# A folding row moved from step 3 to step 4 in an attention and mixture-of-experts kernel, and three smaller edits

## The chip, the cores and the metric

The kernel runs on one core of a Trainium2 chip. The metric is the device time of one execution in microseconds. The engines are TensorE (PE, with its weight loads as PEld), VectorE (DVE), ScalarE (ACT), GpSimd (POOL) and SyncE (SP), which issues most DMAs. Each engine works through its own instructions in order; semaphores hold an instruction until what it needs is there.

## What is computed

Two softmax attentions in a row, through 32 packed rows for each head, and behind them a mixture of four experts:

```python
# q, k, v: (8, 8, 576, 64), p: (8, 8, 32, 64)
p_packed = sm_attn(p, k, v)             # softmax(p k^T / 8) v
attn = sm_attn(q, p_packed, p_packed)   # softmax(q p_packed^T / 8) p_packed
x = attn.transpose(0, 2, 1, 3).reshape(8 * 576, 512)
dp = domain_probs / (domain_probs.sum(-1, keepdims=True) + 1e-09)
out = 0
for e in range(4):                      # w1: (4, 512, 1024), w2: (4, 1024, 512)
    out += dp[:, e:e + 1] * (np.maximum(x @ w1[e], 0.0) @ w2[e])
```

## The kernel before

**Numbers in two parts.** The matmuls run on fp32 values split in a high part (a cast on ACT, L105) and a low part (value minus high part, L109, on DVE or POOL). A product of two such values is three matmuls: high by high and the two mixed ones.

**Folding.** The second attention's output is a softmax matrix times the 32 packed values of each head, and the next step multiplies it by `w1`. The kernel multiplies the packed values by `w1` first. `g_form` (L294) does that for one chunk of 512 hidden columns and for two batches: per pair of heads (g = 0, 1) one matmul group L76 (`wraw` holds `w1`, `ppbd` the packed values) into one PSUM buffer that holds both batches, then, for each batch, the high part on ACT and the low part on DVE, into an SBUF tile `ghl`. Such a step is called a folding row or a fold; a *joined* fold does g = 0 and g = 1 in one stretch of PE and takes two PSUM buffers, otherwise there are two rows with one buffer each.

**Units.** The work behind it is 64 units u: four sweeps (`sb`) of two batches each, eight chunks (`ch`) in a sweep, the two batches in turn. So sweeps begin at u = 0, 16, 32 and 48. A unit runs seven steps i = 0 to 6 (L657 to L692). Each step has a product: 12 matmuls of the unit's second matrix multiplication in a Strassen form with seven products (`product`, L459), added into `acc` i on DVE (L477). With it comes an operand for a product two steps later (`s_operand`, L365): an add on DVE for some (`sblk`, L375), a high part on ACT, a low part on POOL (`st`). At i = 1, 3, 4 and 6 a *group* of 12 matmuls of the next unit's first matrix multiplication follows (`mm1_groups`, L357, operands `xh`, `xl`, `ghl`), read out by DVE (L350, rectified and weighted, into `ablk`). Behind it, at some steps, a fold is done.

**What sets the order.** PE's order is written out by the code. All of `dbl`, the products, the groups, the folds, and attention's scores and transposes, take turns in one pool of four PSUM buffers (L54), so the fifth taker waits until the first buffer has been read out. The order of the other engines between fixed points is found by a scheduler from the program's dependencies, when the kernel is built; `after` (L59) pins one instruction behind another on an engine. At run time each engine keeps to that order.

**Attention for the next sweep** (scores L76 with `kt`, `pt`; transposes L71; softmax on DVE and ACT; `back`, L680) is spread over the units of the present sweep, at even steps, behind the fold of the same step. At the end of a sweep the seven accumulators are combined (L508, on DVE and POOL) and stored, spread over the next unit's steps (`sums`, L683).

**The folds' places now** (L633 to L637 and L669): from u = 4 on, in every even unit. In the first sweep there are two rows, behind the groups of steps 3 and 6, except u = 14, which prepares the second sweep and is joined, behind step 6. From u = 16 to u = 58 all are joined, behind the group of step 3. u = 60 is joined, behind step 0. The tiles `ghl` come from five buffers, every sixth from a sixth one (`ghl6`, L288).

**The end.** The last unit forms its result by quarters (`quadrant`, L438). The last quarter, (1, 1), is stored in two halves j = 0 and 1 (L451, L452), both out of one PSUM tile.

Of the kernel before, what the change touches and what calls it, by code (L numbers as in the profile page):

```python
# [9 lines left out]
F32R = mybir.dt.float32r  # L10
# [6 lines left out]
P = 128  # L17
# [4 lines left out]
NG = NPAIR // 2  # L22
SB = B // 2
HS = S // 2
FC = 512
NCH = E * F // FC
# [14 lines left out]
def attention_moe(ctx: ExitStack, tc: tile.TileContext, q, k, v, p, dp, w1, w2, out):  # L41
    nc = tc.nc

    def pool(name, bufs=1, **kw):
        return ctx.enter_context(tc.tile_pool(name=name, bufs=bufs, **kw))
# [4 lines left out]
    gpool = pool("gpool")  # L50
# [8 lines left out]
    def after(ins, prev):  # L59
        tc.add_manual_dep(ins, prev.name, nosync, reason="order on an engine")  # L60
# [6 lines left out]
    def mm(**kw):  # L67
        on_pe(nc.tensor.matmul(**kw))  # L68
# [15 lines left out]
    def dbl():  # L84
        return ps_dbl.tile([P, 2, 512], F32, name="dbl")
# [12 lines left out]
    def cols(b, hh):  # L98

        i = (hh + b) % 2  # L100
        return slice(i * NPK, (i + 1) * NPK)

    def hi_of(dst, src, eng):
        if eng is nc.scalar:
            return nc.scalar.copy(out=dst, in_=src)  # L105
        return eng.tensor_copy(out=dst, in_=src)
# [116 lines left out]
    marks = {}  # L223
# [59 lines left out]

    gs = {}

    ring = {"n": 0}

    def ghl_tile():  # L288
        n, ring["n"] = ring["n"], ring["n"] + 1
        if n % 6 == 0:  # L290
            return glast.tile([P, 2, FC], F32R, name="ghl6")
        return gpool.tile([P, 2, FC], F32R, name="ghl", bufs=5)

    def g_form(bs, ch, raws, rows=None, tile=lambda: gpool.tile([P, 2, FC], F32R, name="ghl", bufs=5)):  # L294

        for gr in rows or [[g] for g in range(NG)]:
            pss, calls = {}, []
            for g in gr:
                ps = dbl()
                pss.update({(b, g): ps[:, b % 2] for b in bs})  # L300
                for hs in range(4):
                    pr, hh = 2 * g + hs // 2, hs % 2
                    part = slice(hh * D, (hh + 1) * D)
                    for b in bs:
                        c0 = (hs // 2) * 2 * NPK + cols(b, hh).start
                        calls.append(dict(
                            out=pss[b, g][c0:c0 + NPK, :], lhsT=ppbd[b % 4][part, pr, cols(b, hh)],
                            rhs=raws[pr][part, :], start=True, stop=True,
                        ))
            together(calls)  # L310
            for b in bs:
                for g in gr:
                    ghl = tile()
                    hi_of(ghl[:, 0, :], pss[b, g], nc.scalar)
                    marks[b, ch, g, "low"] = lo_of(ghl[:, 1, :], pss[b, g], ghl[:, 0, :], nc.vector).ins
                    gs.setdefault((b, ch), []).append(ghl)
            yield
# [5 lines left out]
    AHEAD = LAST - 3  # L323
# [114 lines left out]
    def quadrant(r, n):  # L438
        sb, ch, b = units[LAST]
        right = ((0, "b12"), (6, 5))  # L440
        ps = dbl()
        t = accs[b, ORDER.index({(0, 0): "a12", (0, 1): "s4", (1, 0): "a22", (1, 1): "s1"}[r, n])]
        for j in range(2):
            terms = [(k, fi, tl, sl) for k in range(2) for fi in range(2) for tl, sl in ((0, 0), (1, 0), (0, 1))]
            for m, (k, fi, tl, sl) in enumerate(terms):
                mm(
                    out=ps[:, j, 0:HS], lhsT=tt[ch, right[k][n]][:, tl, fi, j * P:(j + 1) * P],
                    rhs=blocks[LAST, "op", 2 * r + k][:, sl, fi, :], start=m == 0, stop=m == len(terms) - 1,
                )
            if (r, n) == (1, 1):  # L450
                nc.vector.tensor_tensor(out=t[:, j], in0=ps[:, j, 0:HS], in1=t[:, j], op=ALU.add)  # L451
                (nc.sync, nc.scalar)[j].dma_start(  # L452
                    out=out[n * DH + j * P:n * DH + (j + 1) * P, b * S + r * HS:b * S + (r + 1) * HS], in_=t[:, j],
                )
        if (r, n) != (1, 1):
            nc.vector.tensor_tensor(out=t, in0=ps[:, :, 0:HS], in1=t, op=ALU.add)
            store(b, t, r, n)
# [72 lines left out]
    def drain(gen):  # L530
        for _ in gen:
            pass
# [5 lines left out]
    with ExitStack() as first:  # L538
# [20 lines left out]
        raws = w1_load(0)  # L559
# [18 lines left out]
        raws = w1_load(1)  # L578
# [34 lines left out]
    for u, (sb, ch, b) in enumerate(units):  # L613
        odd = b % 2 == 1
        nxt = units[u + 1] if u + 1 < len(units) else None

        step = 2 * ch + b % 2
        if sb + 1 < SB:
            pair = [2 * sb + 2, 2 * sb + 3]
            for at_step, make, g in AT_FIRST if sb == 0 else AT_LATER:  # L620
                if at_step == step:
                    drain(back)
                    back = make(pair, g, att_tile, relief=sb == 0)

        gsteps = nothing
        nsb, nch = (sb, ch + 1) if ch + 1 < NCH else (sb + 1, 0)
        if u == 0:
            gsteps = g_form([0], 1, raws)
        elif u == 2 or u == 3:
            gsteps = g_form([1] if u == 2 else [0, 1], u - 1, raws)  # L630
            drain(gsteps)
            raws = w1_load(u)
        elif 3 < u <= AHEAD and not odd and nsb < SB:  # L633
            whole = dict(rows=[range(NG)]) if nsb > 0 else {}
            if sb > 0:
                whole["tile"] = ghl_tile
            gsteps = g_form([2 * nsb, 2 * nsb + 1], nch, raws, **whole)  # L637
        if u == 2 * NCH - 1:
            later.close()
            glast = later.enter_context(tc.tile_pool(name="glast", bufs=1, reuse_waits="tile"))  # L640
        elif u == LAST - 1:
            extra = plain_operand(NCH - 1)
            next(extra)
        elif u == LAST:
            for _ in combine(b, SUMS_LAST):
                pass
            for r in range(2):
                for n in range(2):
                    quadrant(r, n)
                    if r == 0:  # L650
                        s_operand(u, LA + n)
            break
        forming = u == 0 or u > 2 and odd and sb == 0 and ch + 1 < NCH
        if forming:
            tsteps = t_form(ch + 1, raw_tile, {"t1": nc.gpsimd, "t2": nc.vector, "t3": nc.vector, "t4": nc.gpsimd})
            next(tsteps)
        for i in range(NPROD):  # L657
            product(u, i)
            n = i + LA
            if n < NPROD:  # L660
                s_operand(u, n)
            elif nxt:
                s_operand(u + 1, n - NPROD)
            if nxt:
                for grp in (GROUPS_LATE if u in (1, AHEAD) else GROUPS_LAST if u == LAST - 1 else GROUPS).get(i, ()):
                    mm1_groups(u + 1, [grp])
            if u == 0:
                drain(gsteps)
            elif i in ((0,) if u == AHEAD else (6,) if u == 2 * NCH - 2 else (3, 6)):  # L669
                next(gsteps, None)  # L670
            if u == 1 and i == 3:
                drain(second)
                drain(g_form([1], 0, raws))
                raws = w1_load(1)
            for _ in range(SECOND[u][i] if u in SECOND and i < len(SECOND[u]) else 0):
                next(second, None)
            if i == 4 and u > 1 and u + 2 < len(units) and units[u + 2][1] % 2 == 0:
                load_probs(units[u + 2][2], units[u + 2][1] // 2)
            if i % 2 == 0 or sb == 0 and step >= AT_FIRST[2][0]:
                next(back, None)  # L680
            if sb == 0 and i in (FORM_ODD if odd or u == 0 else FORM_EVEN):
                next(tsteps, None)
            next(sums, None)  # L683
            if sb == 0 and not odd:
                t_store(ch, i)
            if u == LAST - 1:
                if i == 1:
                    next(extra)
                elif i in (0, 5, 6):
                    t_load(nxt[1], i)  # L690
            elif nxt and not forming and nxt[1] != ch:
                t_load(nxt[1], i)  # L692
        drain(gsteps)
        drain(sums)
        if ch == NCH - 1:
            sums = combine(b, SUMS)
        if u == 0:
            raws = w1_load(0)
            load_probs(1, 0)
        elif not odd and u > 2:  # L700
            nsb, nch = (sb, ch + 2) if ch + 2 < NCH else (sb + 1, ch + 2 - NCH)
            if nsb < SB:
                raws = w1_load(nch)
# [34 lines left out]
```

## Time and profile before

| | |
|---|---|
| median of three runs | 1296.7 us (1296.26 to 1297.26) |
| profiled execution | 1296.23 us |
| its span, first to last instruction | 1294.4 us |
| DVE busy | 954.9 us (74%) |
| POOL busy | 859.3 us (66%) |
| ACT busy | 493.3 us (38%) |
| PE line of the products, L68 dbl<-st,tt | 5388 matmuls, 772.2 us busy |
| PE line of the folds, L76 dbl<-wraw,ppbd | 1024 matmuls, 69.6 us busy |
| chain that ended last | PE 82%, POOL 7%, DVE 6%, DMA 3%, issue 2%, ACT 1% |

The busy time of an engine says only how much work it has. What a change can win or lose is read from where PE waits, and from what ends that wait. In a timeline row stand the start in us, the duration, the engine, the line, the operation, the written and the read tile with their shapes, how many instructions are drawn together, and in brackets how long the engine was idle before and what ended that idle time.

### The profile page before, as it was taken

To read this page: it belongs to the slowest core of one execution; us is meant where nothing else is said; L and a number is where in the kernel's file an instruction comes from. 1 tells how busy PE (TensorE), PEld (TensorE's weight loads), DVE (VectorE), ACT (ScalarE), POOL (GpSimd) and SP (SyncE) were. 2 spreads that over 40 slices of the span, in tenths; PEclk is the share of its full clock that TensorE was granted. 3 is DMA by queue.
4 is the path that set the end of the run, shared out by engine and by line. 5 is a ranking of instruction groups with operands and counts; after the bars stand their busy time and mean duration, and the time that the engine had idled before them with its cause. 6 is when DMAs were issued, how large, how long until landed. Compare 5 with 4: busy or idle time off the path is not lost.

```text
span 1294.4 us, 26901 instructions
## 1 busy us (share of the span) xinstructions
PE 1265.8 (98%) x10776; PEld 1179.6 (91%) x10776; DVE 954.9 (74%) x1304; ACT 493.3 (38%) x884; POOL 859.3 (66%) x570
## 2 busy tenths in 40 slices
PE   7899999999999999999999999999999999999998
PEld 4689999998889999999999999999999999999998
DVE  6786677899975666897686666799669566766776
ACT  3445545646344333333324423333323533332321
POOL 4778888798985444666578454466567755555565
PEclk9999999999999999999999999999999999999999
DMA  9885656544365544544345546434436443443562
GB/s 351 308 294 195 219 169 228 181 148 167 141 234 198 157 157 129 191 161 156 126 138 187 179 142 201 139 130 124 156 124 202 155 135 115 128 153 130 169 210 97
DMA packets 91707, 223.93 MB, mean 173 GB/s; under 512 B 9280, under 2 KB 32192, under 8 KB 91584
## 3 DMA queue, kind: packets, MB, share of 16 engines
q1 hardware_dynamic: 90768, 221.92, 51.4%
q8 instruction: 86, 1.41, 0.5%
q10 hardware_dynamic: 816, 0.30, 0.1%
q14 instruction: 37, 0.30, 0.1%
HBM read 183.31 MB, written 38.87 MB: 172 GB/s over the span
## 4 chain that ended last, share of the span: by engine, by line
PE 82%; POOL 7%; DVE 6%; DMA 3%; issue 2%; ACT 1%; SPq 0%; DVEq 0%; POOLq 0%; ACTq 0%
PE dbl L68 76%; PE dbl L76 5%; POOL st L109 3%; POOL tt L109 2%; DVE sblk L375 2%; DVE ablk L350 1%; DVE ghl L109 1%; DMA xl<-in_q 1%; POOL b L412 1%; POOL acc L508 1%; DVE a L264 1%; PE dbl L71 1%; DMA vt<-in_v 1%; DMA kt<-in_q 0%; DVE acc L477 0%
## 5 line engine op out<-in xcount | busy, mean ns | idle before, releaser
L68 PE MATMUL dbl<-st,tt 128*128 128x288 f32 x5388 | 772.2, 297 | 7.1 <-POOL st L109 2.1
L68 PEld LDWEIGHTS dbl<-st,tt 128*128 128x128 f32 x5388 | 730.1, 188 | 48.2 <-issue 27.4
L109 POOL TENSOR_TENSOR st<-sblk,st 128x576 fp32r<-128x576 f32 x252 | 393.6, 1569 | 234.4 <-ACT st L105 192.4
L68 PE MATMUL dbl<-xh,ghl 128*128 128x288 f32 x2048 | 415.8, 295 | 5.8 <-DVE ghl L109 3.5
L109 POOL TENSOR_TENSOR st<-ablk,st 128x576 fp32r<-128x576 f32 x193 | 291.0, 1511 | 152.5 <-ACT st L105 151.1
L477 DVE TENSOR_TENSOR acc<-dbl,acc 128x576 f32<-128x576 f32 x385 | 288.3, 752 | 113.7 <-PE dbl L68 113.2
L68 PEld LDWEIGHTS dbl<-xh,ghl 128*128 128x128 f32 x2048 | 328.3, 188 | 7.6 <-DVE ghl L109 4.4
L350 DVE SCALAR_TENSOR_TENSOR ablk<-dbl,pbt 128x576 f32<-128x576 f32 x256 | 192.4, 753 | 156.0 <-PE dbl L68 151.6
L68 PE MATMUL dbl<-xl,ghl 128*128 128x288 f32 x1024 | 300.9, 294 | 1.0 <-DVE xl L109 1.0
L105 ACT CAST st<-sblk 128x576 fp32r<-128x576 f32 x252 | 170.3, 676 | 298.4 <-DVE sblk L375 205.7
L105 ACT CAST st<-ablk 128x576 fp32r<-128x576 f32 x193 | 130.3, 675 | 264.4 <-PE dbl L68 242.2
L68 PEld LDWEIGHTS dbl<-xl,ghl 128*128 128x128 f32 x1024 | 192.1, 188 | 1.4 <-DVE xl L109 1.4
L375 DVE TENSOR_TENSOR sblk<-ablk 128x576 f32<-128x576 f32 x126 | 126.1, 1001 | 9.2
L105 ACT CAST ghl<-dbl 128x512 fp32r<-128x512 f32 x128 | 72.7, 586 | 84.6 <-PE dbl L76 51.9
L109 DVE TENSOR_TENSOR ghl<-dbl,ghl 128x512 fp32r<-128x512 f32 x128 | 85.1, 684 | 11.0 <-ACT ghl L105 8.5
L375 DVE TENSOR_TENSOR sblk<-ablk,sblk 128x576 f32<-128x576 f32 x63 | 69.8, 1107 | 5.7
L76 PE MATMUL dbl<-wraw,ppbd 64*32 64x512 f32 x1024 | 69.6, 596 | 0.4 <-DMA wraw<-in_w 0.3
L109 POOL TENSOR_TENSOR tt<-b,tt 128x512 fp32r<-128x512 f32 x42 | 62.2, 1489 | 2.1 <-ACT tt L105 2.0
L375 DVE TENSOR_TENSOR sblk<-sblk,ablk 128x576 f32<-128x576 f32 x63 | 57.7, 915 | 1.7
L508 POOL TENSOR_TENSOR acc<-acc,acc 128x576 f32<-128x576 f32 x28 | 47.0, 1686 | 11.4 <-DVE acc L477 11.4
L475 ACT COPY acc<-dbl 128x576 f32<-128x576 f32 x56 | 35.9, 640 | 46.4 <-PE dbl L68 46.3
L508 DVE TENSOR_TENSOR acc<-acc,acc 128x576 f32<-128x576 f32 x28 | 39.1, 1400 | 4.9 <-POOL acc L508 4.6
(91 smaller groups left out, 432.9 us busy)
## 6 DMA issues: line engine op xcount, KB each, us to landing
tt<-td SPq DMA_DIRECT2D x192, 512.0 KB, 4.2
wraw<-in_w SPq DMA_DIRECT2D x136, 256.0 KB, 3.8
td<-tt SPq DMA_DIRECT2D x56, 512.0 KB, 3.5
pbt<-pnd SPq DMA_DIRECT2D x32, 288.0 KB, 4.1
out<-acc SPq DMA_DIRECT2D x31, 288.0 KB, 2.3
kt<-in_k SPq DMA_DIRECT2D x14, 576.0 KB, 5.3
kt<-in_q SPq DMA_DIRECT2D x14, 576.0 KB, 5.4
vt<-in_v SPq DMA_DIRECT2D x15, 512.0 KB, 5.3
```

The lines of the kernel that those rows point to most:

```text
L68: on_pe(nc.tensor.matmul(**kw))
L71: on_pe(nc.tensor.transpose(**kw))
L76: ins = nc.tensor.matmul(**kw).ins
L105: return nc.scalar.copy(out=dst, in_=src)
L109: return eng.tensor_tensor(out=dst, in0=src, in1=hi.bitcast(F32), op=ALU.subtract)
L264: marks[b, g, "mul"] = eng.tensor_tensor(out=a2, in0=a2, in1=s2.broadcast_to([P, S // 32, NPK]), op=ALU.mult).ins
L350: nc.vector.scalar_tensor_tensor(out=a, in0=ps[:, :, 0:HS], scalar=0.0, in1=pbt[b][:, c * HS:(c + 1) * HS].rearrange("p (o t) -> p o t", o ...
L375: nc.vector.tensor_tensor(out=t, in0=blk(x), in1=blk(y), op=op)
L412: eng[m].tensor_tensor(out=blk[place], in0=blk[x], in1=blk[y], op=ALU.subtract)
L475: nc.scalar.copy(out=accs[b, i], in_=psv)
L477: nc.vector.tensor_tensor(out=accs[b, i], in0=psv, in1=accs[b, i], op=ALU.add)
L508: eng.tensor_tensor(out=m[dst], in0=m[x], in1=m[y], op=op)
```

## The change

From u = 18 to u = 58 the joined fold is done behind the group of step 4 instead of step 3. In u = 14 and u = 16 it is no longer joined: two rows, behind the groups of steps 3 and 6. Within a fold the high and low parts are now issued with g outside and the batch inside, and the tile that goes to `ghl6` is given by the fold's turn instead of a counter. In u = 12, one multiplication of attention's softmax is pinned behind the low part of a fold. In the last quarter, the second half gets a PSUM tile of its own.

```diff
-    def ghl_tile():
-        n, ring["n"] = ring["n"], ring["n"] + 1
-        if n % 6 == 0:
+    def g_tile(kept=False):
+        if kept:
             return glast.tile([P, 2, FC], F32R, name="ghl6")
         return gpool.tile([P, 2, FC], F32R, name="ghl", bufs=5)
...
-            for b in bs:
-                for g in gr:
-                    ghl = tile()
+            tiles = {(b, g): g_tile((b - bs[0], g) == kept) for b in bs for g in gr}
+            for g in gr:
+                for b in bs:
+                    ghl = tiles[b, g]
                     hi_of(ghl[:, 0, :], pss[b, g], nc.scalar)
...
         for j in range(2):
+            if (r, n, j) == (1, 1, 1):
+                ps = dbl()
...
-            whole = dict(rows=[range(NG)]) if nsb > 0 else {}
+            how = {}
             if sb > 0:
-                whole["tile"] = ghl_tile
-            gsteps = g_form([2 * nsb, 2 * nsb + 1], nch, raws, **whole)
+                turn = (u - 2 * NCH) // 2
+                how["kept"] = (1, 0) if turn == 0 else (None, (0, 1), (1, 1))[(turn - 1) % 3]
+                if turn > 0:
+                    how["rows"] = [range(NG)]
+            gsteps = g_form([2 * nsb, 2 * nsb + 1], nch, raws, **how)
...
-            elif i in ((0,) if u == AHEAD else (6,) if u == 2 * NCH - 2 else (3, 6)):
+            elif i in ((0,) if u == AHEAD else (4,) if u > 2 * NCH else (3, 6)):
                 next(gsteps, None)
...
         drain(gsteps)
+        if u == 12:
+            after(marks[2, 1, "mul"], marks[0, 7, 0, "low"])
```

How that moves instructions is shown at u = 36, in the third sweep. Two lines taken out ahead of these places make line 375 into 373 and line 350 into 348 in the changed kernel. First DVE. Before, from the eviction of the group of step 3 (L350) on: one add, the four low parts with accumulation 4 among them, the eviction of the group of step 4, two adds, then the maxima of attention's scores (L172).

```order
L350 SCALAR_TENSOR_TENSOR ablk<-dbl,pbt 128x576
L375 TENSOR_TENSOR sblk<-ablk 128x576
L109 TENSOR_TENSOR ghl<-dbl,ghl 128x512
L109 TENSOR_TENSOR ghl_9764<-dbl,ghl_9764 128x512
L109 TENSOR_TENSOR ghl<-dbl,ghl 128x512
L477 TENSOR_TENSOR acc_8779<-dbl,acc_8779 128x576
L109 TENSOR_TENSOR ghl<-dbl,ghl 128x512
L350 SCALAR_TENSOR_TENSOR ablk<-dbl,pbt 128x576
L375 TENSOR_TENSOR sblk<-ablk 128x576
L375 TENSOR_TENSOR sblk<-sblk,ablk 128x576
L172 TENSOR_REDUCE nb<-dbl 128x1 x2
L176 TENSOR_SCALAR nb<-nb 128x1
```

Now, from the same eviction on:

```order
L348 SCALAR_TENSOR_TENSOR ablk<-dbl,pbt 128x576
L373 TENSOR_TENSOR sblk<-ablk 128x576
L477 TENSOR_TENSOR acc_8749<-dbl,acc_8749 128x576
L348 SCALAR_TENSOR_TENSOR ablk<-dbl,pbt 128x576
L373 TENSOR_TENSOR sblk<-ablk 128x576
L373 TENSOR_TENSOR sblk<-sblk,ablk 128x576
L109 TENSOR_TENSOR ghl<-dbl,ghl 128x512 x4
L172 TENSOR_REDUCE nb<-dbl 128x1 x2
L176 TENSOR_SCALAR nb<-nb 128x1
L477 TENSOR_TENSOR acc_8814<-dbl,acc_8814 128x576
```

The four low parts have moved behind the eviction of the group of step 4 and behind two adds instead of one, in front of L172. The `acc` rows count from accumulation 4 (8779 before, 8749 now) to accumulation 5 (8814).

On PE at the same fold, from its last two matmuls on (`ppbd_83` and `ppbd_84` are the packed values of the two batches, `xh_6608` and `xl_6609` the high and low part of a group's operand, `kt,pt` attention's scores). Before, product 4 and its group follow:

```order
L76 MATMUL dbl<-wraw,ppbd_83 32x512
L76 MATMUL dbl<-wraw,ppbd_84 32x512
L68 MATMUL dbl<-st,tt 128x288 x12
L68 MATMUL dbl<-xh_6608,ghl 128x288 x2
L68 MATMUL dbl<-xl_6609,ghl 128x288
```

Now the scores follow, then products 5 and 6, then the group of step 6:

```order
L76 MATMUL dbl<-wraw,ppbd_83 32x512
L76 MATMUL dbl<-wraw,ppbd_84 32x512
L76 MATMUL dbl<-kt,pt 32x288 x16
L68 MATMUL dbl<-st,tt 128x288 x24
L68 MATMUL dbl<-xh_6608,ghl 128x288 x2
```

What attention puts at step 4 of a unit, scores here and transposes in others, used to stand one product and one group behind the fold and now stands straight behind it.

More of the change, by code (lines that the diff above doesn't have):

```diff
@@ L284, in attention_moe, with g_form @@
     gs = {}
-    ring = {"n": 0}
-    def ghl_tile():
-        n, ring["n"] = ring["n"], ring["n"] + 1
-        if n % 6 == 0:
+    def g_tile(kept=False):
+        if kept:
             return glast.tile([P, 2, FC], F32R, name="ghl6")
         return gpool.tile([P, 2, FC], F32R, name="ghl", bufs=5)
-    def g_form(bs, ch, raws, rows=None, tile=lambda: gpool.tile([P, 2, FC], F32R, name="ghl", bufs=5)):
+    def g_form(bs, ch, raws, rows=None, kept=None):
         for gr in rows or [[g] for g in range(NG)]:
```

## The prediction

> **What bounds the kernel now.** I read the page first, then what TensorE waited for, then the order of events around single folds, because the change moves folds.
>
> ```profile
> span 1294.4 us, 26901 instructions
> PE 1265.8 (98%) x10776; PEld 1179.6 (91%) x10776; DVE 954.9 (74%) x1304; ACT 493.3 (38%) x884; POOL 859.3 (66%) x570
> PEclk9999999999999999999999999999999999999999
> ```
>
> PE is busy for 98% of the span and its clock is full in every slice. PE is the path: 28.6 us (1294.4 - 1265.8) are all that moving work could give, and any new wait of PE is paid in full. The change adds or drops no instruction of PE's arithmetic, so the forecast is a sum of waits. From 300 us on, where the change acts, PE waited for:
>
> ```profile
> PE dbl L68 <- DVE ghl L109: 2.9, 2, 1.7
> PE dbl L68 <- issue: 1.7, 2, 1.1
> PE dbl L68 <- DVE ablk L350: 1.5, 1, 1.5
> PE dbl L68 <- DVE nb L176: 0.9, 1, 0.9
> ```
>
> (total, times, longest, in us). These are few. Below I price a wait by the start-to-start time of PE's groups against an undisturbed one, which is slightly more than the idle time that a row shows.
>
> **A fold now and later, at a plain place.** This is the fold of u=50, at step 3, with no attention work near it:
>
> ```profile
> 1045.68 1.95 PE L76 MATMUL dbl<-wraw,ppbd 64*32 64x512 f32 x32
> 1045.79 0.76 DVE L350 SCALAR_TENSOR_TENSOR ablk<-dbl,pbt 128x576 f32<-128x576 f32 x1 [0.84 <-PE dbl L68]
> 1046.65 0.76 DVE L375 TENSOR_TENSOR sblk<-ablk 128x576 f32<-128x576 f32 x1
> 1047.56 1.87 PE L68 MATMUL dbl<-st,tt 128*128 128x288 f32 x12
> 1049.27 0.43 PE L68 MATMUL dbl<-xh,ghl 128*128 128x288 f32 x2
> 1050.87 2.29 PE L68 MATMUL dbl<-st,tt 128*128 128x288 f32 x16
> ```
>
> Call the fold's start F. The fold takes 1.88 us (1047.56 - 1045.68), the product behind it 1.71, the group 1.60. A fold fills two of the four PSUM buffers, so the third 12-matmul piece behind it takes the fold's first buffer again and must wait until both low parts in it are made. Now that is product 5, at F+5.19. On DVE, eviction L350 runs at F+0.11, one add L375 from F+0.97 to F+1.73, then the lows. How they follow one another in the g-first order, which the change writes down, is seen at u=36, together with what comes behind:
>
> ```profile
> 776.37 0.69 DVE L109 TENSOR_TENSOR ghl<-dbl,ghl 128x512 fp32r<-128x512 f32 x1
> 777.10 1.08 ACT L105 CAST ghl<-dbl 128x512 fp32r<-128x512 f32 x2 [0.76 <-DVE ghl L109]
> 777.72 1.29 DVE L109 TENSOR_TENSOR ghl<-dbl,ghl 128x512 fp32r<-128x512 f32 x2 [0.65 <-ACT ghl L105]
> 779.80 1.20 PE L76 MATMUL dbl<-kt,pt 64*32 64x288 f32 x32
> 780.93 3.47 PE L68 MATMUL dbl<-st,tt 128*128 128x288 f32 x24
> 781.12 1.19 DVE L375 TENSOR_TENSOR sblk<-ablk 128x576 f32<-128x576 f32 x1
> 783.09 1.42 DVE L172 TENSOR_REDUCE nb<-dbl 128x1 f32<-128x576 f32 x2
> 785.28 0.53 PE L68 MATMUL dbl<-xh,ghl 128*128 128x288 f32 x2 [0.88 <-DVE nb L176]
> ```
>
> The second cast waits for the first low (777.10 behind 776.37 + 0.69), the second low starts 1.35 us behind the first, the third 0.65 later. At step 4 the new DVE order has group 4's eviction and then **two** adds ahead of the lows. Two such adds of one step, undisturbed, stand at u=20:
>
> ```profile
> 469.33 0.76 DVE L375 TENSOR_TENSOR sblk<-ablk 128x576 f32<-128x576 f32 x1
> 469.49 3.47 PE L68 MATMUL dbl<-st,tt 128*128 128x288 f32 x24
> 470.19 0.76 DVE L375 TENSOR_TENSOR sblk<-sblk,ablk 128x576 f32<-128x576 f32 x1
> 473.06 0.54 PE L68 MATMUL dbl<-xh,ghl 128*128 128x288 f32 x2
> ```
>
> They start 0.86 apart. So at step 4 the adds end at F+2.59, low 1 starts at F+2.60, low 2 at F+3.95 and ends at F+4.60, low 3 ends at F+5.25, and low 4, behind its cast (half of the row's 1.08) and mostly behind one accumulation of 0.75, at about F+6.60.
>
> How long PE takes to go on after a low is seen at u=24, one of four places (549, 588, 861 and 900 us) where a fold holds PE up now:
>
> ```profile
> 547.40 0.43 PE L68 MATMUL dbl<-xh,ghl 128*128 128x288 f32 x2
> 548.39 1.29 DVE L109 TENSOR_TENSOR ghl<-dbl,ghl 128x512 fp32r<-128x512 f32 x2 [0.66 <-ACT ghl L105]
> 549.34 2.89 PE L68 MATMUL dbl<-st,tt 128*128 128x288 f32 x20 [0.18 <-PE dbl L68]
> ```
>
> Low 2 ended at 549.04; PE went on 0.3 later. I use 0.25. The group there took 1.94 instead of 1.60, a wait of 0.34.
>
> Behind a step-4 fold come products 5 and 6 (3.28 for the two, below) and group 6, at F+5.16; it needs low 2, free at F+4.85. At the **nine plain folds** (u=22, 28, 38, 44, 50 to 58) the margin falls from over 1 us to 0.3, and the change is worth 0. That cover is thin: each 0.3 us lost on DVE uses it up.
>
> **Folds with transposes behind them (u=18, 34).**
>
> ```profile
> 429.41 0.71 PE L71 MATMUL dbl<-ident,a 128*128 128x128 f32 x5
> 429.87 3.44 PE L68 MATMUL dbl<-st,tt 128*128 128x288 f32 x24
> 433.15 0.43 PE L68 MATMUL dbl<-xh,ghl 128*128 128x288 f32 x2
> ```
>
> Five transposes take 0.46 of PE, two products 3.28. The transposes also take a PSUM buffer. Before, they came behind group 4, some 5 us after the fold. Now they come straight behind it, so the fold's first buffer is asked for one piece sooner, by product 6: F+1.88+0.46+1.64 = F+3.98, but free at F+4.85: wait 0.87. Group 6 then would start at F+6.49 and needs low 4 (F+6.60+0.25; here I take F+6.95 because low 4's queue has acc5 ahead): wait 0.46. Together 1.33 a fold, **+2.65** for two; between 0 (lows in time) and 2 x 1.8 (adds at the 1.19 of the row above).
>
> **Folds with scores behind them (u=20, 36).** The scores take 1.13 of PE (779.80 to 780.93) and two buffers, so product 5 already asks for the fold's first one: F+3.01 against F+4.85, wait 1.84. Product 6 asks for the second: F+6.49 against F+6.85, wait 0.36. Group 6 asks for a scores buffer, free 2.19 us after the two L172 begin (785.28 - 783.09); they now stand behind low 4, so F+6.63+2.19 = F+8.82 against F+8.49: 0.33. Together 2.53, and the waits of the present go: 785.28 - 780.93 - 3.28 = 1.07 at u=36 and 473.06 - 469.49 - 3.28 = 0.29 at u=20. **+3.7** for both (between -1.36, if the lows come in time and nothing new appears, and +5).
>
> **Folds with attention's elementwise work near (u=24, 26, 40, 42).** The 0.34 waits go, 1.36 in all, since the transpose of attention's tile stays at step 3. But it delays accumulation 4, and all DVE work behind it by about 0.5, which puts the release at F+5.35 against F+5.16. I take **0** for the four; ends -1.36 and +2.4.
>
> **Folds at the sweeps' ends (u=30, 32, 46, 48).** Here a sum (L508) stands in DVE's queue:
>
> ```profile
> L508 DVE TENSOR_TENSOR acc<-acc,acc 128x576 f32<-128x576 f32 x28 | 39.1, 1400 | 4.9 <-POOL acc L508 4.6
> ```
>
> A 1.40 us piece ahead of the lows uses up the margin of 0.3 where it falls between fold and low 2. I take 0.3 a fold, **+1.2**; ends 0 and 4 x 1.1 (1.40 - 0.30). The two waits marked "issue" (product 2 of u=32 and u=48, behind such sums) stay.
>
> **Units 12 to 16.**
>
> ```profile
> 311.85 1.09 PE L76 MATMUL dbl<-wraw,ppbd 64*32 64x512 f32 x16
> 312.87 3.45 PE L68 MATMUL dbl<-st,tt 128*128 128x288 f32 x24
> ...
> 356.86 1.83 PE L68 MATMUL dbl<-st,tt 128*128 128x288 f32 x12 [1.46 <-DVE ablk L350]
> 359.93 0.53 PE L68 MATMUL dbl<-xh,ghl 128*128 128x288 f32 x2 [1.23 <-DVE ghl L109]
> ```
>
> The wait at 359.93 (3.07 instead of 1.71: 1.36) is for u=14's joined fold, the four lows of which come at once; after the split only two remain behind step 6, and I let it go. The other two now fall into DVE's stretch from 341 to 356 us, which already makes PE wait: +0.5 taken, between 0 and 1.4. A half fold takes 1.02 (312.87 - 311.85), two 2.04 against 1.88: +0.16, twice (u=14, u=16). Sum **-0.5**, ends -1.4 and +0.7. The pin for u=12 asks for an order of DVE that the program has already (low ahead of multiplication; DVE's rows up to u=14 are the same in both): 0. The longest wait on a low, 1.7 us at 319 us, stays. wraw's loads go out earlier at u=14 and 16 and one step later from u=18 on; the row that they serve is a whole unit pair away, so I cost them 0, and a late one would cost PE what it is late.
>
> **The tail.**
>
> ```profile
> 1283.83 4.83 PE L68 MATMUL dbl<-st,tt 128*128 128x288 f32 x35
> 1288.70 0.46 DVE L451 TENSOR_TENSOR acc<-dbl,acc 128x288 f32<-128x288 f32 x1 [0.84 <-PE dbl L68]
> 1289.21 1.86 PE L68 MATMUL dbl<-st,tt 128*128 128x288 f32 x12 [0.55 <-DVE acc L451]
> ```
>
> The last 12 matmuls wait for the eviction of the first half from the same tile. With a tile of their own they follow at once: **-0.6** (the idle 0.55 and the overlap of two matmuls). Nothing else is late there, and the end of the kernel comes that much sooner.
>
> **Sum.** 2.65 + 3.7 + 0 + 1.2 - 0.5 - 0.6 = +6.45 us on the profiled execution's 1296.23, that is 1302.7. The median of the three runs is 0.47 above that execution and their spread is 1.0, so I leave it there.
>
> **A rule against the change.** The add L375 with both inputs in SBUF takes 0.76 where POOL is still and 1.19 at 781.12, while POOL was in an operation; over the kernel:
>
> ```profile
> L375 DVE TENSOR_TENSOR sblk<-ablk 128x576 f32<-128x576 f32 x126 | 126.1, 1001 | 9.2
> ```
>
> The mean is 1.00. [...]
>
> **Rivals.** (1) *Faster:* the lows come early enough everywhere, because DVE makes them ahead of the point where PE asks. This decides at the step-4 folds: low 2 would have to end by F+2.8 at u=20 and by F+3.7 at u=18. Then the waits of the present go: -1.36 (four folds) -1.36 (u=20, 36) -1.36 (359.93) +0.32 -0.6 = -4.4, 1291.9. For it: DVE is busy only 74%, and each of these waits is real. Against: two adds ahead of the lows in DVE's order. (2) *Stretched adds:* if the adds at each fold take 1.19, low 2 comes 0.43 later: 0.13 at nine plain folds, 0.43 at the other twelve, +6.3: 1309. For it the mean of 1.00; against, the adds at u=50 and u=20 took 0.76. (3) *It cancels:* waits at u=18 to 36 about half as long as worked out (+3.2), the sweeps' ends +0, the four folds -1.36, the rest -1.1: +0.7, 1297. (4) *The moved fold changes nothing* because the scheduler places it elsewhere: excluded, the order of PE shows it behind group 4; the pin at u=12 is the part that does nothing.
>
> **Chances.** Forecast (1299 to 1306) 0.42, stretched adds 0.07, cancelling 0.23, faster 0.28. A measurement of this kernel tells about 0.2%, 2.6 us. So faster by more 0.28, within 0.23, slower 0.49. Signs are mixed, so the range goes over both: 1291 to 1309; the forecast's own is 1299 to 1306.
>
> **What would show it.** Right: PE's waits at the step-4 folds of u=18, 20, 34 and 36, named after DVE's ghl low and nb, with DVE's lows behind two adds; no waits at product 5 of u=24, 26, 40, 42; no wait at L451; the wait at 319 us unchanged; none on a low at about 360 us. Wrong: no PE wait behind the folds of u=20 and u=36 (rival 1), or waits at plain folds such as u=50 (rival 2), or new waits for wraw.

## The result and the profile after

| | before | changed |
|---|---|---|
| median | 1296.48 us (6 runs, 1295.51 to 1298.04) | 1307.17 us (6 runs, 1305.44 to 1308.25) |
| ratio to before | | 1.0081, 95% interval 1.0068 to 1.0094 |
| profiled execution, its span | 1296.23, 1294.4 us | 1308.18, 1306.4 us |

The change costs 10.7 us (0.8%). The page of the changed kernel (span, busy times, granted clock of TensorE in 40 slices):

```profile
span 1306.4 us, 26921 instructions
PE 1268.6 (97%) x10776; PEld 1182.4 (91%) x10776; DVE 971.8 (74%) x1304; ACT 491.6 (38%) x884; POOL 859.1 (66%) x570
PEclk9999999999999999999999999999999999999999
```

Of the 12.0 us of span, PE's busy time has 2.8, the rest is new idle time of PE. What PE waited for from 300 us on (total, times, longest):

```profile
PE dbl L68 <- DVE ghl L109: 13.5, 14, 2.0
PE dbl L68 <- issue: 2.2, 2, 1.1
PE dbl L68 <- POOL st L109: 1.1, 4, 0.4
PE dbl L68 <- DVE ablk L348: 0.2, 1, 0.2
```

The waits on a fold's low parts have gone from 2.9 to 13.5 us. The lines of DVE's acc L451 (the tail) and nb L176 are gone.

To place the difference I took the start of each unit's first product in both traces and their difference (every unit has 84 matmuls `dbl<-st,tt`, in the same order in both). From u = 12 on it changes by more than 0.2 us only where something was changed; from u = 50 to u = 63 it is flat at 12.76 us:

| where | forecast, us | in the profiled executions, us |
|---|---|---|
| ahead of u = 12 (nothing changed there) | 0 | +1.1 |
| u = 14 to 18 | -0.5 | -1.65 |
| u = 18, 34 (transposes behind the fold) | +2.65 | +1.46 |
| u = 20, 36 (scores behind the fold) | +3.7 | +3.79 |
| u = 24, 26, 40, 42 | 0 | +2.69 |
| u = 30, 32, 46, 48 (sweeps' ends) | +1.2 | +5.4 |
| nine plain folds | 0 | 0 |
| tail | -0.6 | -0.82 |

The first row is how two executions differ at their start, which the medians do not carry. The fold of u = 24, which I had costed at nothing, as a timeline:

```profile
549.60 0.74 DVE L348 SCALAR_TENSOR_TENSOR ablk<-dbl,pbt 128x576 f32<-128x576 f32 x1
550.26 1.42 POOL L109 TENSOR_TENSOR st<-sblk,st 128x576 fp32r<-128x576 f32 x1
550.37 1.92 DVE L373 TENSOR_TENSOR sblk<-ablk 128x576 f32<-128x576 f32 x1
552.32 0.76 DVE L373 TENSOR_TENSOR sblk<-sblk,ablk 128x576 f32<-128x576 f32 x1
553.00 0.68 DVE L109 TENSOR_TENSOR ghl<-dbl,ghl 128x512 fp32r<-128x512 f32 x1
554.34 1.29 DVE L109 TENSOR_TENSOR ghl<-dbl,ghl 128x512 fp32r<-128x512 f32 x2 [0.65 <-ACT ghl L105]
555.17 0.51 PE L68 MATMUL dbl<-xh,ghl 128*128 128x288 f32 x2 [0.83 <-DVE ghl L109]
```

The fold began at 549.00. Two adds stand ahead of the lows, as the order had shown, and the first takes 1.92 us and not 0.76, beside a POOL operation that began 0.1 us ahead of it. Low 2 ends at about 554.98, F+5.98 where the plain fold at 1061.64 has F+4.53 (1066.17), and group 6 waits. At the sweeps' ends both adds are longer, at u = 30 (1.26 and 1.80 us):

```profile
665.02 1.26 DVE L373 TENSOR_TENSOR sblk<-ablk 128x576 f32<-128x576 f32 x1
665.62 1.96 POOL L109 TENSOR_TENSOR st<-sblk,st 128x576 fp32r<-128x576 f32 x1
666.38 1.80 DVE L373 TENSOR_TENSOR sblk<-sblk,ablk 128x576 f32<-128x576 f32 x1
```

At u = 32 it is above all the second add:

```profile
705.36 1.95 POOL L109 TENSOR_TENSOR st<-sblk,st 128x576 fp32r<-128x576 f32 x1
706.13 1.80 DVE L373 TENSOR_TENSOR sblk<-sblk,ablk 128x576 f32<-128x576 f32 x1
710.02 0.50 PE L68 MATMUL dbl<-xh,ghl 128*128 128x288 f32 x2 [0.51 <-DVE ghl L109]
```

At u = 36, where scores follow the fold, nothing is stretched, and PE waits 1.87 us (1.97 at u = 20, the longest):

```profile
785.82 0.76 DVE L373 TENSOR_TENSOR sblk<-ablk 128x576 f32<-128x576 f32 x1
786.68 0.76 DVE L373 TENSOR_TENSOR sblk<-sblk,ablk 128x576 f32<-128x576 f32 x1
787.35 0.68 DVE L109 TENSOR_TENSOR ghl<-dbl,ghl 128x512 fp32r<-128x512 f32 x1
788.69 1.29 DVE L109 TENSOR_TENSOR ghl<-dbl,ghl 128x512 fp32r<-128x512 f32 x2 [0.65 <-ACT ghl L105]
789.63 5.02 PE L68 MATMUL dbl<-st,tt 128*128 128x288 f32 x24 [1.87 <-DVE ghl L109]
```

The fold began at 784.85: lows from F+2.50, release of PE at F+4.78, against F+2.60 and F+4.85 worked out. But the 24 matmuls take 5.02 us instead of 3.47. The windows behind the wait show why (stretch and its length, busy times of PE, PEld, DVE, ACT and POOL with the number of instructions, then the granted clock, the DMA share and GB/s):

```profile
790.00:792.00 2.00, 2.00 (x14) 1.88 (x13) 1.37 (x3) 0.72 (x2) 0.00 (x0) 0.73 0.97 272
792.00:794.00 2.00, 2.00 (x10) 2.00 (x10) 1.58 (x5) 1.80 (x4) 1.38 (x1) 0.50 0.98 398
```

The granted clock of TensorE was 0.50 from 790.93 to 794.34 us. The page's row PEclk, in tenths, hides that. The tail is as forecast, 61 matmuls in one row, the first half read out while the second runs:

```profile
1294.72 8.29 PE L68 MATMUL dbl<-st,tt 128*128 128x288 f32 x61
1301.45 0.46 DVE L451 TENSOR_TENSOR acc<-dbl,acc 128x288 f32<-128x288 f32 x1 [0.84 <-PE dbl L68]
```

### The profile page after: what moved, and what is told of

It is laid out like the page before. It is cut to its first block, busy times and chain, and to the rows that moved or that the text cites. A ratio compares the mean times of both kernels' runs of the same rounds, so it can differ in the third digit from the quotient of the medians.

```text
span 1306.4 us, 26921 instructions
## 1 busy us (share of the span) xinstructions
PE 1268.6 (97%) x10776; PEld 1182.4 (91%) x10776; DVE 971.8 (74%) x1304; ACT 491.6 (38%) x884; POOL 859.1 (66%) x570
## 3 DMA queue, kind: packets, MB, share of 16 engines
q8 instruction: 86, 1.41, 0.4%
## 4 chain that ended last, share of the span: by engine, by line
PE 67%; DVE 14%; POOL 12%; issue 3%; DMA 2%; ACT 2%; SPq 0%; DVEq 0%; ACTq 0%; POOLq 0%
PE dbl L68 63%; POOL st L109 7%; DVE sblk L373 5%; PE dbl L76 3%; DVE ablk L348 2%; DVE ghl L109 2%; POOL tt L109 2%; DVE acc L477 2%; POOL acc L508 1%; POOL xl L109 1%; POOL b L410 1%; DMA xl<-in_q 1%; DVE a L238 1%; ACT ghl L105 1%; DVE a L252 1%
## 5 line engine op out<-in xcount | busy, mean ns | idle before, releaser
L109 POOL TENSOR_TENSOR st<-ablk,st 128x576 fp32r<-128x576 f32 x193 | 296.3, 1539 | 131.6 <-ACT st L105 128.6
L348 DVE SCALAR_TENSOR_TENSOR ablk<-dbl,pbt 128x576 f32<-128x576 f32 x256 | 192.1, 752 | 151.1 <-PE dbl L68 149.9
L373 DVE TENSOR_TENSOR sblk<-ablk 128x576 f32<-128x576 f32 x126 | 126.5, 1005 | 9.2
L373 DVE TENSOR_TENSOR sblk<-ablk,sblk 128x576 f32<-128x576 f32 x63 | 82.0, 1302 | 5.5
L373 DVE TENSOR_TENSOR sblk<-sblk,ablk 128x576 f32<-128x576 f32 x63 | 61.4, 975 | 3.0
L508 POOL TENSOR_TENSOR acc<-acc,acc 128x576 f32<-128x576 f32 x28 | 46.0, 1653 | 18.7 <-DVE acc L477 18.6
L508 DVE TENSOR_TENSOR acc<-acc,acc 128x576 f32<-128x576 f32 x28 | 41.4, 1482 | 4.1 <-POOL acc L508 3.7
```

The source lines that it names most:

```text
L109: return eng.tensor_tensor(out=dst, in0=src, in1=hi.bitcast(F32), op=ALU.subtract)
L348: nc.vector.scalar_tensor_tensor(out=a, in0=ps[:, :, 0:HS], scalar=0.0, in1=pbt[b][:, c * HS:(c + 1) * HS].rearrange("p (o t) -> p o t", o ...
L373: nc.vector.tensor_tensor(out=t, in0=blk(x), in1=blk(y), op=op)
L508: eng.tensor_tensor(out=m[dst], in0=m[x], in1=m[y], op=op)
```

## The experiments

Nine kernels ran. Each is compared with the kernel before, run beside it on the same chip (medians 1296.35 or 1296.37 us).

**The move undone, all else kept.**

```diff
-            elif i in ((0,) if u == AHEAD else (4,) if u > 2 * NCH else (3, 6)):
+            elif i in ((0,) if u == AHEAD else (3, 6)):
```

> The changed kernel with the joined folds of u=18 to u=58 back at step 3; all other edits stay. Theory (the move alone costs: DVE makes the low parts behind two adds, while PE asks for the PSUM buffers sooner): the waits behind the twelve folds near attention or sums (13.2 us by the units' starts) go, the gains at u=14 to 16 (1.6) and in the tail (0.7 to 0.8) stay: 1294 us, 2.3 below before. Rival (the new order of the low parts within a fold, the new turn of ghl6 or the two split folds cost it): 1300 us or more.

Measured: 1293.67 us (10 runs), ratio 0.9980 (0.9970 to 0.9989). The move alone makes the loss; without it the rest of the change is a gain of 2.7 us. By the units' starts the gain is made at u = 14 to 18 (-1.65) and in the tail; u = 48's wait named "issue" also shrinks by 0.63. One thing goes the other way, +0.79 at u = 20, where this kernel has the low parts g-first and the kernel before had them batch by batch (that this order is the reason was not tried alone):

```profile
471.85 0.54 PE L68 MATMUL dbl<-xh,ghl 128*128 128x288 f32 x2 [0.89 <-DVE nb L176]
```

**The move alone.** The kernel before, with `(4,) if u > 2 * NCH` put ahead of `(3, 6)` in its own line.

> The kernel before, with nothing changed but the joined folds of u=18 to u=58 at step 4. Theory: all of the loss and none of the gains: 1296.5 + 13.2 = 1309.7 us, with waits of PE on low parts behind the same twelve folds. Rival (order of the low parts, split, tiles): 1303 us or less.

Measured: 1307.35 us (4 runs), ratio 1.0082 (1.0065 to 1.0099). PE's waits:

```profile
PE dbl L68 <- DVE ghl L109: 13.6, 13, 2.0
```

The waits stand behind the same twelve folds. The time is 2.3 below the expected 1309.7. So the move cost 11.0 us here and 13.5 on top of the other edits; the two kernels differ by 0.2 in their medians, though the gains at u = 14 to 18 and in the tail should set them 2.5 apart. By the units' starts 0.8 of that is given back at u = 48, 0.24 at u = 34; the rest lies within the spread of each (2.6 and 2.8 us) and I did not follow it up.

**The adds behind the lows.**

```diff
-            nc.vector.tensor_tensor(out=t, in0=blk(x), in1=blk(y), op=op)
+            add = nc.vector.tensor_tensor(out=t, in0=blk(x), in1=blk(y), op=op).ins
+            if name in ("s1", "s2") and 2 * NCH < u - 1 < AHEAD and (u - 1, "fold") in blocks:
+                after(add, blocks[u - 1, "fold"])
...
+        if 3 < u <= AHEAD and not odd and nsb < SB:
+            blocks[u, "fold"] = marks[2 * nsb + 1, nch, NG - 1, "low"]
```

> The changed kernel with one more pin: the two adds that the next unit needs (s1, s2) stand behind the last low part of the fold on DVE. Theory (the adds ahead in DVE's queue set the waits): low 2 ends about F+3.9 instead of F+4.6 to F+5.8; PE's waits at u=24, 26, 30, 32, 40, 42, 46 and 48 go (about 8 us), at u=18 and 34 they fall from 0.72 to 0.2 or less, at u=20 and 36 from 2.0 to 1.1: 1296 to 1298.5 us. Rival (the waits are for PSUM's turn alone and stay, or the late adds hold up the next unit's products): 1303 us or more.

Measured: 1296.62 us (10 runs), ratio 1.0001 (0.9992 to 1.0010), within what was expected. With the fold still at step 4, the adds' place in DVE's queue alone takes 10.5 us back. The waits at u = 18, 24, 26, 34, 40 and 42 are gone; at u = 20 and 36 1.2 us on the lows and 0.7 behind the scores' maxima stay. The fold's waits at u = 30, 32, 46 and 48 went too, but the adds, later now, push the rest of DVE's queue, and a wait of 0.72 us (idle) appears in u = 31 and 47:

```profile
669.10 1.99 DVE L510 TENSOR_TENSOR acc<-acc,acc 128x576 f32<-128x576 f32 x1
671.01 0.74 DVE L348 SCALAR_TENSOR_TENSOR ablk<-dbl,pbt 128x576 f32<-128x576 f32 x1
672.41 0.79 PE L68 MATMUL dbl<-st,tt 128*128 128x288 f32 x4 [0.72 <-DVE acc L479]
```

(L510 and L479 are the sums and accumulations, lines 508 and 477 elsewhere.)

**Transposes ahead of the fold, u = 18 and 34.**

```diff
+            if u in (18, 34) and i == 4:
+                next(back, None)
             if u == 0:
...
-            if i % 2 == 0 or sb == 0 and step >= AT_FIRST[2][0]:
+            if (i % 2 == 0 or sb == 0 and step >= AT_FIRST[2][0]) and not (u in (18, 34) and i == 4):
```

> The changed kernel with attention's transposes of u=18 and u=34 ahead of the fold of step 4 instead of straight behind it; PE's work and DVE's order are the same. Theory (a PSUM taker straight behind the fold brings the request for the fold's first buffer forward by one piece): DVE's lows end at the same time, but the first buffer is asked for by group 6 and not by product 6, so the two waits of 0.72 us go, 1.4 less: 1305.7 us. Rival (DVE is late whoever asks): waits of 0.5 or more stay at both.

Measured: 1305.36 us (2 runs), ratio 1.0067 (1.0049 to 1.0085). Both waits are gone; the units behind start 0.73 earlier each. DVE's order and the lows' distance from the group are the same, so what PE asks for first is what made these two waits. Some 0.2 comes back one unit later at each.

**No POOL operation beside the add: a miss, and again.**

```diff
-        lo_of(st[:, 1], src, st[:, 0], nc.gpsimd)
+        if u in (24, 26, 40, 42) and i == 5:
+            nc.scalar.copy(out=st[:, 1], in_=src)
+        else:
+            lo_of(st[:, 1], src, st[:, 0], nc.gpsimd)
```

> The changed kernel, with the low part of one operand (product 5 of u=24, 26, 40, 42) written by ACT as a copy of the value instead of by POOL; this part of the computation is left out. POOL then has no add to do while DVE does the first of the two adds of step 4. Theory (the adds are stretched beside POOL): that add falls from 1.92 to about 0.76 us at these four folds and the waits of 1.0 there go: 4 us less, about 1303. Rival (the number of entries in DVE's queue, whatever POOL does): the adds stay above 1.5 us or the waits above 0.5: 1305 us or more.

Measured: 1305.16 us (2 runs). I had taken the wrong operand: a POOL operation still stood beside the add, which took 1.91 us at u = 24, and the idle times fell only from about 0.85 to 0.36 us, since other work on DVE ended sooner. That decides nothing about the stretched add. It does show what the delay ahead of it is worth: at u = 24 the eviction L348 began at F+0.11 and not at F+0.60, and the four units behind start 0.45 to 0.53 sooner. The second try has the condition `u in (25, 27, 41, 43) and i == 1`.

> As the run before of this kind, but with the right POOL operation: the low part of the next unit's operand 1 (units 25, 27, 41, 43) is a copy by ACT, and left out as a low part; it is the POOL operation that starts 0.1 us ahead of the first add of step 4 at u=24, 26, 40, 42. DVE's order is the same row by row. Theory (stretched adds): that add falls from 1.92 to 0.76 us, the four waits of 1.0 go: about 4 us less, 1303. Rival (the queue's length alone): the add stays long or the waits stay above 0.5.

Measured: 1302.69 us (2 runs), ratio 1.0046 (1.0028 to 1.0065). The same place at u = 24:

```profile
550.04 0.76 DVE L373 TENSOR_TENSOR sblk<-ablk 128x576 f32<-128x576 f32 x1
552.84 1.29 DVE L109 TENSOR_TENSOR ghl<-dbl,ghl 128x512 fp32r<-128x512 f32 x2 [0.65 <-ACT ghl L105]
553.83 0.43 PE L68 MATMUL dbl<-xh,ghl 128*128 128x288 f32 x2
```

DVE's order is the same row by row, one POOL operation is gone, the add takes 0.76 and PE does not wait. At all four folds the next unit starts 1.06 to 1.10 sooner, relative to the changed kernel. The stretched add is the cause there. This is the mechanism of rival 2 of the prediction, at four folds, and with a longer add (1.92 us) than the 1.19 that the rival went by.

**Step 4 without u = 20 and 36.** The condition becomes `u > 2 * NCH and u not in (20, 36)`.

> The changed kernel with only u=20 and u=36 back at step 3. Theory: the two waits of 2 us on lows go, and with them the stretches in which the clock was granted at 0.5 (some 3 us behind the wait at 789.6 us in the changed kernel's profile): 1307.2 - 2 x 1.8 and up to 1 us more for each such stretch: 1302 to 1303.6 us, mean clock 0.999 or 1 in all executions, and a smaller spread than 2.8 us. Rival (the clock dips are not tied to these waits): clocks of 0.994 to 0.997 stay.

Measured: 1304.59 us (4 runs), ratio 1.0062 (1.0047 to 1.0078). It is 1 us above the expected range: at step 3, g-first, u = 20 waits 0.89 us on nb as in the first experiment. The waits of 2 us and the half clock behind them are gone from the profile (granted clock 1.00 from 470 to 480 and from 790 to 800 us). But the mean clocks are still 0.996 to 1: this profile has its clock of 0.83 and 0.89 at 10 to 20 and 30 to 40 us, at the program's start. The kernel before, which has no such waits, had means of 0.996 to 1 in its nine executions beside this kernel. So the mean clock of a run does not tell the two apart, and that part of the expectation was wrong.

**Step 3 with pins.** The move undone, and three kinds of pins on DVE:

```diff
...
+            if name == "s3" and u in (25, 27, 41, 43):
+                sb, ch, b = units[u - 1]
+                after(add, marks[2 * sb + 1, ch + 1, 1, "low"])
+            if name == "s1" and u in (21, 37):
+                after(add, marks[2 * units[u][0] + 2, 1, "nb"])
...
-        if u == 12:
-            after(marks[2, 1, "mul"], marks[0, 7, 0, "low"])
+        if u == 13:
+            after(marks[3, 1, "mul"], marks[0, 7, 1, "low"])
```

> Fold at step 3, the other edits kept, and three kinds of pins on DVE that put work behind what PE waits for: (a) at u=24, 26, 40, 42 the add of step 3 behind the fold's lows (PE waits 0.35 each there), (b) at u=20 and 36 the next unit's two adds behind the maxima of the scores (0.9 and 1.05), (c) the pin at u=12 put on the other batch's multiplication and the low part that PE really waits for at 319 us (1.86). Theory (DVE's order is what makes each of these waits): all seven go: 1293.7 - 1.4 - 1.9 - 1.8 = 1288.6 us. Rival (the waits only move to the next thing that DVE then has late): 1291.5 or more.

Measured: 1290.32 us (5 runs), ratio 0.9952 (0.9939 to 0.9964). (b) gave 1.17 and 1.15. (c) gave 0.9 of 1.86: the low part is in time, and PE now waits for the accumulation behind the multiplication. (a) gave nothing; the four waits stayed, for another reason:

```profile
541.30 0.78 DVE L269 STREAM_TRANSPOSE at<-a 128x576 f32<-128x576 f32 x1
542.11 0.67 ACT L105 CAST xh<-at 128x576 fp32r<-128x576 f32 x1 [2.14 <-DVE at L269]
542.69 0.58 ACT L105 CAST ghl<-dbl 128x512 fp32r<-128x512 f32 x1
543.30 0.69 DVE L109 TENSOR_TENSOR ghl<-dbl,ghl 128x512 fp32r<-128x512 f32 x1 [1.22 <-ACT ghl L105]
```

DVE is idle 1.22 us for the fold's cast, and that stands on ACT behind a cast that waits for DVE's transpose; ACT itself was idle 2.14 us in front of it.

**The fold's casts first.**

```diff
...
+        if u in (24, 26, 40, 42):
+            after(marks[2 * sb + 3, u // 2 % 2, "high"], marks[2 * sb + 1, ch + 1, 0, "cast"])
```

> As the run with the pins at step 3, and at u=24, 26, 40 and 42 one pin more, on ACT: the cast of attention's tile (xh) stands behind the cast of the fold's second tile. There the waits of 0.35 us stayed, though no add stood ahead of the lows on DVE any more. Theory: the first low waited for ACT's cast, and that stood behind a cast which waits for DVE's transpose (542.11 behind 541.30 + 0.78); with the fold's casts first the first low starts about 1.2 us sooner and the four waits go: 1.4 us less, 1288.9. Rival (the transpose on DVE alone sets it): the waits of 0.35 stay, 1290.3.

Measured: 1288.46 us (4 runs), ratio 0.9938 (0.9921 to 0.9955). Each of the four units behind starts 0.41 to 0.43 earlier. This version is 8 us faster than the kernel before and 19 faster than the changed one.

## Why the prediction was right, and where its sizes were off

The forecast was slower by 6.45 us (1302.7), and the measured loss is 10.7 (1307.17). The mechanism that it named, low parts that come late behind two adds, is the one that the runs show. Its sizes were off in both directions: the forecast's own range, 1299 to 1306, does not hold 1307.17, and the range over both signs does so only because it reaches to the stretched adds (1309), to which I gave 0.07. In the profiled executions the eight folds near attention's elementwise work and at the sweeps' ends, where adds stretch, cost 8.1 us against a forecast of 1.2, while the folds with scores or transposes and units 14 to 18 together came out 2.2 below their terms. Point by point:

- *PE is the path and a new wait is paid in full.* Right: the units' starts move by each wait and do not come back (0.18 us at u = 47 apart).
- *The move costs, the small edits gain.* Shown by the first two experiments: 13.5 or 11.0 us for the move, -2.7 for the rest.
- *Two adds ahead of the lows.* Shown by pinning them behind: 10.5 us come back with the fold at step 4. Where nothing is stretched, the lows started within 0.1 us of the time worked out, and the nine plain folds made no wait, as forecast.
- *Scores behind the fold (+3.7).* Size right, in part by chance. Without the half clock the two folds cost 1.80 and about 1.03 (as u = 36 does in the run of the move alone, where the granted clock was 1.00 from 790 to 796 us), and the half clock, which was in no term, added nearly 1 us at u = 36. The first of the three waits worked out was there (1.97 and 1.87 us, worked out 1.84), of the two behind it (0.36 and 0.33) at most 0.2 was: at u = 20 products 5 and 6 took 3.67 us together instead of 3.47, and group 6 began with no wait at 475.07, when ACT was still reading the scores (475.11 for 0.74 us). So it did not take a scores buffer, which the prediction had it wait for.
- *Transposes behind the fold (+2.65).* The cause is shown by putting them ahead. The wait of product 6 was right (0.72, worked out 0.87). The second, 0.46 at group 6, was not there: the step that failed is that buffers go strictly in turn, as the section on the kernel before says too. The last low part ends at 433.37. Group 6 begins 0.02 us before that; in this trace's sixteen waits of over 0.1 us on a fold's low part PE went on 0.05 to 0.35 us behind that part's end:

```profile
432.68 0.69 DVE L109 TENSOR_TENSOR ghl<-dbl,ghl 128x512 fp32r<-128x512 f32 x1
433.35 0.43 PE L68 MATMUL dbl<-xh,ghl 128*128 128x288 f32 x2
```

  In the program's dependencies group 6 takes the buffer of the transposes, which ACT frees early, and the fold's second one goes to a later piece.
- *u = 24, 26, 40, 42 (0, measured +2.69)* and *the sweeps' ends (+1.2, measured +5.4).* These terms were mis-sized. I used the adds' undisturbed 0.76 us and an allowance of 0.5 us for a delay of accumulation 4, and held stretched adds for a rival with a chance of 0.07, although the page's mean of 1.00 spoke for it. At the first four the stretched add is shown to be the cause by taking its POOL neighbour away. At the sweeps' ends the prediction took a sum L508 in DVE's queue for the reason; in the changed kernel's rows none stands on DVE between the fold and its low 2, but two stretched adds do (1.26 and 1.80 at u = 30 and 46, 0.89 and 1.80 at u = 32 and 48). With the adds behind the lows these four waits go. The "issue" wait at u = 32 is also longer (1.10, before 0.53). I did not try these parts one by one.
- *Units 14 to 16 (-0.5, measured -1.65).* The allowance of 0.5 for the two moved lows was not needed: PE's idle times between 343 and 360 us fell from 3.55 us together to 1.18. But I had forecast that none on a low would be left there, and one of 0.64 us (idle) is, at 359.91. *The tail (-0.6, measured -0.82)* and *the pin at u = 12 (0)* held: the wait of 1.7 us at 319 us is still there, and moves when the pin is put on the other batch's multiplication.
- *Signs.* PE's waits at u = 18, 20, 34 and 36 came, named after the lows; none on nb came. Those at u = 24, 26, 40 and 42 came at group 6, and none at product 5. Waits at plain folds, the sign for rival 2, did not come: there the adds took 0.76 us.

## What to carry to other kernels

Work that PE must have read out soon belongs ahead of work that is needed later, in the queue of each engine on its way: here pins of a few adds and casts were worth more than moving the matmuls. Before moving a piece on a saturated engine, count which engines' queues it lands behind, and price the neighbours' operations by what they take beside each other, not by what they take alone (one add here: 1.92 us beside POOL, 0.76 alone). When a pin brings nothing, look at the operand's other engine: the head of that queue may wait for something else.

## What the runs showed of the hardware

The adds L373 on DVE, with both inputs in SBUF, took longer beside POOL's work. In the changed kernel's trace, the 96 with POOL still take 0.74 to 0.76 us; the 125 that lie beside POOL's work for over half of their time have a median of 1.32 and go up to 2.06. The 240 evictions L348 beside POOL's work, with one input in PSUM, take 0.71 to 0.76. Taking one POOL operation away brought an add from 1.92 back to 0.76. In this trace each of the 115 adds that began while a POOL operation had more than 0.2 us left (0.24 to 1.37) ended 0.61 to 0.63 us behind that operation's end. (At u = 24 above, POOL's ends at 551.68 and the add at 552.29.) POOL's operations took longer too when the add was first: the 66 low parts `st` that began while an add had more than 0.2 us left took 1.75 to 2.03 us, the one at 665.62 among them 1.96; the one at 550.26, ahead of its add, takes 1.42, and the 276 with no such add beside them take 1.41 to 2.05, with a median of 1.44. The runs show these times, not what makes them.

Behind an idle time of PE of 1.87 us, which ended at 789.63, the granted clock was 0.50 from 790.93 to 794.34 us. It fell to 0.50 in some other executions too, behind the like wait at u = 20:

```profile
470.00:480.00 10.00, 8.03 (x63) 7.70 (x48) 6.91 (x17) 4.63 (x11) 2.85 (x2) 0.83 0.69 229
```

That is the kernel with the move alone; 0.83 is the mean granted clock of these 10 us. In the changed kernel's own profile, u = 20 had a wait of 1.97 us and a granted clock of 1.00 from 470 to 480 us, and the idle times of 1.7 us at 319 us had 1.00 from 310 to 330 us in the profiles of both kernels. So the stretch behind the wait at u = 36 cost nearly 1 us more (3.79 - 1.80 - 1.03 by the units' starts), and the wait at u = 20 had no such stretch. In front of both waits stand only the matmuls of the fold and the scores, on tiles of 64*32, for 2.9 us (784.85 to 787.76 at u = 36). What decides it in an execution was not tried.
